# Rescheduling VectorE's work on batch 1 inside batch 0: fold pieces, evictions and two additions moved

## The chip, the cores and the metric

One core of a Trainium2 chip. The time is the device time of one execution in microseconds (us).

## The reference, cut to what matters

```python
X = np.fft.fft(np.fft.fft(x, axis=1), axis=2).real      # x: 8 x 3008 x 256
h = np.maximum(X^T @ w_tok1, 0) @ w_tok2                 # token mixing, per batch
u = X + h^T
out = u + np.maximum(u @ w_ch1, 0) @ w_ch2               # channel mixing, 1536 hidden
```

## The kernel before

Everything runs on TensorE as matmuls: the Fourier transform (`z`, `w`, `y`), the token product (`pt`, `pu`), the first channel product (`pc`) and the second (`po`, or seven products of half size, `pa` and `pb`). Other names in the traces: `ut` is the addition of token product and transform, on VectorE; `pad` is the last piece of the folded rows; `s` are sums of `c`, the evicted first product, for the seven products; a bank is one of the buffers into which TensorE writes, and an eviction empties it. The main loop goes through slots. A slot is one block of 128 hidden channels of the first channel product for one chunk of 512 rows; a chunk has 12 slots, a batch 72. Between the products of batch b the loop puts pieces of batch b+1's **front** (its transform and token mixing), and for batch 0 also what is left of its own front (`own`). Batch 1's rows must first be **folded** (sums and differences of mirrored rows): 26 pieces on VectorE in slots 12 to 29.

```python
for t0 in (11, 6, 1):                       # front: z from the folded rows eo
    for half in range(2):
        pz = ps_f("pz")
        ...
        copy(half == 0 and b > 0, zo[:, :, :, t0:t0 + 5], ...)   # True: VectorE, False: ScalarE
        yield
...
tt(ut[...], pu[...], yv, AT.add)            # token product + transform -> u, on VectorE
...
own_at = {..., 12: 1, 15: 1, 18: 1, 20: 1, 22: 1, 24: 1, 27: 1, 30: 1, 33: 1, 36: 1, 39: 1}
for b in range(BB):
    first = 24 if b == 0 else ...
    for c in range(NCH):
        on_v = ((1, 5, 8), ())[c] if b == 0 and c < 2 else () if joins else (0, 3, 6, 9)
        for ct in range(NCT):
            slot = NCT * c + ct
            mm1(b, c, c1, ct, on_v)         # two matmuls of 512 columns, one eviction with Relu
            ...                             # second product of the chunk before
            take(own, own_at.get(slot, 0))
            if 12 <= slot < 30:
                take(fold1, 1 + slot % 2)   # fold of batch 1
            if slot == 29:
                load_x(2)                   # GpSimd: loads of batch 2
            if 30 <= slot < 34:
                G.tensor_copy(out=w2r[...], in_=w2v[0][...])     # GpSimd: four copies
            while done < NFRONT * (slot + 1 - first) // (71 - first):
                take(nxt, 1)                # front of batch 1
```

Of the kernel before, what the change touches and what calls it, by code (L numbers as in the profile page):

```python
# [36 lines left out]
def kernel(  # L37
# [31 lines left out]
    def ps_f(name, dt=FP32, n=512):  # L69
        return psum.tile([P, n], dt, tag="f", name=name, bufs=3)  # L70
# [24 lines left out]
    def act(out_, in_, scale=1.0, func=AFT.Copy, bias=None):  # L95
        kw = {} if bias is None else {"bias": bias}
        nc.scalar.activation(out=out_, in_=in_, func=func, scale=scale, **kw)  # L97

    def copy(e, out_, in_):
        if e:  # L100
            V.tensor_copy(out=out_, in_=in_)
        else:
            act(out_, in_)
# [32 lines left out]
    def load_x(b):  # L136
        new_x(b)
        load_xp(b)
        for k in range(2):
            load_xm(b, k)  # L140
# [322 lines left out]
    def front(b):  # L463
# [5 lines left out]
        def stage1(out_, rows, half, tab, minus):  # L469
            if b:  # L470
                nc.tensor.matmul(out_, lhsT=rows[:, half * P:half * P + P], rhs=tab,  # L471
                                 start=True, stop=True)
                return
            for k in range(2):
                o = 129 * k + half
                nc.tensor.matmul(out_, lhsT=rows[:, o:o + P], rhs=minus if half and k else tab,
                                 start=k == 0, stop=k == 1)

        for t0 in (11, 6, 1):
            for half in range(2):  # L480
                pz = ps_f("pz")
                for k in range(5):
                    stage1(pz[:, 96 * k:96 * k + 96], eo[:, t0 + k], half, t1r, t1m[:])
                zo = z[:, half, :, :].rearrange("p k (u s) -> p u k s", u=4)
                copy(half == 0 and b > 0, zo[:, :, :, t0:t0 + 5],
                     pz[:, 0:480].rearrange("p (t u k) -> p u k t", t=5, u=4))
                yield
        for half in range(2):
# [10 lines left out]
            zo = z[:, half, :, :].rearrange("p k (u s) -> p u k s", u=4)[:, :, :, 0]  # L499
# [140 lines left out]
    def seven(b, c):  # L640
        if c == NCH - 1:
            return b % 2 == 1 and b < BB - 1
        return b > 0 or c >= 2

    def weight_sums():
        G.tensor_copy(out=wc2[:, :, D:D + 1], in_=wc2[:, :, P:P + 1])
        lo, hi = wc2[:, 0:NH], wc2[:, NH:NCT]
        b12 = lo[:, :, D:P:-1]
        G.tensor_copy(out=b22[:], in_=hi[:, :, D:P:-1])
        tt(t1w[:], b12, lo[:, :, 0:P], AT.subtract, G)  # L650
        tt(t2w[:], b22[:], t1w[:], AT.subtract, G)
        tt(t3w[:], b22[:], b12, AT.subtract, G)
        tt(t4w[:], hi[:, :, 0:P], t2w[:], AT.subtract, G)

    def mm1(b, c, c1, ct, on_v, cts=None):
        ut = state[b]["ut"]
        n = min(CW, S - CW * c)
        cts = cts or (ct,)
        pcs = [ps_out("pc", k % 5) if b + c == 0 and k % 5 < 2 else ps_mm("pc") for k in cts]
        for h in range(2):  # L660
            for pc, ct in zip(pcs, cts):
                nc.tensor.matmul(pc[:, 0:n], lhsT=wc1[:, h, ct * P:(ct + 1) * P],  # L662
                                 rhs=ut[:, c, h, 0:n], start=(h == 0), stop=(h == 1))
        for pc, ct in zip(pcs, cts):
            if ct not in on_v:
                act(c1[:, ct, 0:n], pc[:, 0:n], func=AFT.Relu)
            else:
                ts(c1[:, ct, 0:n], pc[:, 0:n], 0.0, AT.max)
# [3 lines left out]
    def turn_u(b, c):  # L672
        ut = state[b]["ut"]
        uT = work.tile([P, 4, 2, P], FP16, tag="uT", name="uT", bufs=3)
        n = CW if c < 5 or b % 2 else 384
        for h in range(2):
            nc.sync.dma_start_transpose(out=uT[:, 0:n // P, h, :], in_=ut[:, c, h, 0:n])
        return uT
# [18 lines left out]
    def sums(c1, box, k):  # L697
        a11, a12, a21, a22 = quads(c1)
        box[k] = work.tile([P, NH, 2, P], FP16, tag=f"s{k}", name=f"s{k}", bufs=1)
        if k == 1:  # L700
            tt(box[1][:], a21, a22, AT.add)
        elif k == 2:
            tt(box[2][:], box[1][:], a11, AT.subtract)
        elif k == 3:
            tt(box[3][:], a11, a21, AT.subtract)
        else:
            tt(box[4][:], a12, box[2][:], AT.subtract)
# [97 lines left out]
    def take(g, n):  # L805
        for _ in range(n):
            next(g, None)
# [12 lines left out]
    V.memset(td[:, 64:65], 0.0)  # L820
    take(fold0, 5)
    own = front(0)
    take(tu_q, 3)
    take(tu_p, 2)
# [15 lines left out]
    for k in range(4):  # L840
# [12 lines left out]
    hold = const.tile([P, 1], FP16, tag="hold")  # L853
    G.memset(sab[:, :, 1, 0:129:128], 0.0)
    own_at = {1: 1, 2: 1, 4: 1, 12: 1, 15: 1, 18: 1, 20: 1, 22: 1, 24: 1, 27: 1, 30: 1, 33: 1,
              36: 1, 39: 1}
    prev = uT = uT_next = None
    folding = left = 0
    for b in range(BB):
        nxt = front(b + 1) if b + 1 < BB else iter(())  # L860
        fold1 = fold(1, V) if b == 0 and BB > 1 else iter(())
        first, done = (24 if b == 0 else 5 + 12 * ((left + 5) // 6 - 1) if left else 0), 0
        for c in range(NCH):
            c1 = work.tile([P, NCT, CW], FP16, tag="c1", name="c1", bufs=2)
            if c == 5 and b % 2:
                G.tensor_copy(out=c1[:, :, 448:512], in_=tail1[:])
            box = {}
            joins = prev is not None and seven(*prev[0:2])
            on_v = ((1, 5, 8), ())[c] if b == 0 and c < 2 else () if joins else (0, 3, 6, 9)
            for ct in range(NCT):  # L870
                slot = NCT * c + ct
                if b == 0 and slot < 3:
                    if slot == 0:
                        mm1(b, c, c1, ct, on_v, range(3))
                else:
                    mm1(b, c, c1, ct, on_v)
                if b == 0 and slot in (4, 16):
                    uT = turn_u(b, c)
                if ct == (11 if b == 0 and c == 1 else 10) and (b, c) not in ((0, 0), (BB - 1, NCH - 1)):
                    uT_next = turn_u(*divmod(NCH * b + c + 1, NCH))  # L880
                if joins:
                    if ct in places:
                        mm2_seven(*prev, places[ct], pbox)
                    if ct in sum_at:
                        sums(prev[2], pbox, sum_at[ct])
                elif prev is not None and ct % 3 == 2:
                    mm2(*prev, ct // 3, pbox)
                if slot == 1 and b == 0:
                    weight_sums()
                if b == 0:  # L890
                    take(own, own_at.get(slot, 0))
                    if 12 <= slot < 30:
                        take(fold1, 1 + slot % 2)
                    if slot == 29 and BB > 2:
                        load_x(2)
                    if 30 <= slot < 34:
                        th, hb = (slot - 30) // 2, slot % 2
                        G.tensor_copy(out=w2r[:, th, 32 * hb:32 * hb + 32, 0:NQ],
                                      in_=w2v[0][:, th, 32 * hb:32 * hb + 32, :])
                while done < NFRONT * (slot + 1 - first) // (71 - first):  # L900
                    take(nxt, 1)
                    done += 1
                if ct == 5 and (left or done >= 8):
                    if not left and folding < b + 2 < BB:
                        folding, left, fold2 = b + 2, NFOLD, fold(b + 2, G)
                    if left:
                        if joins:
                            G.tensor_copy(out=hold[:], in_=pbox[3][:, 0, 0, 0:1])  # L908
                        n = min(left, 6 if c == 5 or b < 2 else 5)
                        take(fold2, n)  # L910
                        left -= n
                        if left == 0 and folding + 1 < BB:
                            load_x(folding + 1)
            if c == 5 and b % 2 == 0:
                G.tensor_copy(out=tail1[:], in_=c1[:, :, 384:448])
            prev, pbox, uT = (b, c, c1, uT), box, uT_next
# [32 lines left out]
```

## Time and profile before

| | before |
|---|---|
| time, median of 3 | 601.67 us (601.45 to 602.59) |
| TensorE busy | 97% of the span |
| VectorE, ScalarE, GpSimd busy | 75%, 65%, 43% |
| waits of TensorE after slot 0 above 0.3 us, start to start | 1.07 (slot 24), 0.42 (31), 0.59 (39), 0.48 (64) us |

The first matmul of slot 0 starts at 33.63 us; what is before it is setup. A matmul's shown length overlaps the next one's (0.38 us for 512 columns, with the next start 0.215 us on), so a wait of TensorE is read as the distance between two starts less the step that the trace has for that size. The lines of the page and the timelines are in the prediction.

### The profile page before, as it was taken

What the parts mean: (1) busy time and instruction counts of PE and PEld (TensorE: products, weight loads), DVE (VectorE), ACT (ScalarE), POOL (GpSimd) and SP (SyncE); (2) the same over time, 40 slices, a digit from 0 to 9 for tenths busy, and PEclk for the clock granted to TensorE, in tenths of its full rate; (3) what the DMA queues carried; (4) which work ended last, traced back from release to release, by engine and by line L of the source; (5) the groups of instructions that cost most, each with busy time, mean ns of one, the idle gap of its engine ahead of it and who ended that gap; (6) DMA issues with size and microseconds to landing.
All of it is one profiled execution on the core that took longest, in us unless ns stands there. A gap on an engine that the chain in (4) does not pass through costs nothing.

```text
span 599.8 us, 15331 instructions
## 1 busy us (share of the span) xinstructions
PE 582.5 (97%) x6273; PEld 417.8 (70%) x6273; DVE 449.5 (75%) x924; ACT 390.2 (65%) x753; POOL 255.1 (43%) x396
## 2 busy tenths in 40 slices
PE   3899999999999999999999999999999999999997
PEld 3756676677767776667767777677766777666776
DVE  8769879685898668766898668856688757966663
ACT  8764665478647865477656867568665786556662
POOL 8550545937555554626348444565555000000000
PEclk9999999999999999999999999999999999999999
DMA  8992822277138913394335753376133422323533
GB/s 158 207 192 61 170 50 53 61 149 119 37 71 121 149 37 68 78 181 54 68 84 91 135 89 55 67 147 113 37 60 80 93 55 55 77 61 77 93 72 88
DMA packets 83414, 55.69 MB, mean 93 GB/s; under 512 B 53778, under 2 KB 80082, under 8 KB 82578
## 3 DMA queue, kind: packets, MB, share of 16 engines
q1 hardware_dynamic: 76816, 36.82, 31.9%
q0 software_dynamic: 6208, 17.63, 16.2%
q8 instruction: 49, 0.80, 0.6%
q10 hardware_dynamic: 320, 0.26, 0.2%
q14 instruction: 21, 0.17, 0.1%
HBM read 35.26 MB, written 24.64 MB: 100 GB/s over the span
## 4 chain that ended last, share of the span: by engine, by line
PE 82%; DVE 1%; issue 0%; DVEq 0%
PE pc L662 36%; PE pa L712 17%; PE pb L712 13%; PE pu L566 6%; PE po L775 4%; PE pt L595 3%; PE pz L471 1%; PE py L538 1%; PE pw L512 1%; PE pw L508 1%; DVE s L90 1%; DVE osb L90 0%; DVE ut L90 0%; PE pz L496 0%; DVE q L90 0%
## 5 line engine op out<-in xcount | busy, mean ns | idle before, releaser
L97 ACT ACTIVATE c<-pc 128x512 f16<-128x512 f32 (+1 forms) x553 | 314.4, 591 | 156.2 <-PE pc L662 138.7
L662 PE MATMUL pc<-ut,wc 128*128 128x512 f16 (+1 forms) x1152 | 316.5, 374 | 1.2 <-DVE ut L90 1.2
L712 PEld LDWEIGHTS <-s 128*128 128x128 f16 x1968 | 123.5, 98 | 37.5 <-DVE s L90 0.6
L662 PEld LDWEIGHTS <-wc 128*128 128x128 f16 x1152 | 97.0, 98 | 50.7 <-issue 3.0
L712 PEld LDWEIGHTS <-c 128*128 128x128 f16 x1476 | 93.0, 97 | 27.8
L90 DVE TENSOR_TENSOR q<-pa,uT 128x256 f32<-128x256 f32 x123 | 52.5, 427 | 47.6 <-PE pa L712 47.5
L90 DVE TENSOR_TENSOR s<-c 128x1536 f16<-128x1536 f16 x82 | 80.7, 984 | 4.7 <-ACT c L97 4.7
L908 POOL COPY hold<-s 128x1 f16<-128x1 f16 x29 | 5.4, 187 | 173.5 <-DVE s L90 173.5
L90 DVE TENSOR_TENSOR osb<-pb,q 128x256 f32<-128x256 f32 x123 | 52.0, 422 | 23.8 <-PE pb L712 20.3
L90 DVE TENSOR_TENSOR ut<-pu,yt 128x512 f16<-128x512 f32 (+1 forms) x96 | 63.3, 672 | 0.8 <-PE pu L566 0.4
L90 POOL TENSOR_TENSOR eo<-sab 96x512 f16<-96x512 f16 x48 | 52.7, 1114 | 1.6
L566 PE MATMUL pu<-w2r,uu 128*128 128x512 f16 (+1 forms) x168 | 50.0, 379 | 0.3 <-DVE ut L90 0.3
L90 POOL TENSOR_TENSOR sab<-fa,fb 96x256 f16<-96x256 f16 (+1 forms) x72 | 46.7, 673 | 0.0
L90 DVE TENSOR_TENSOR s<-s,c 128x1536 f16<-128x1536 f16 x41 | 40.4, 986 | 0.0
L97 ACT ACTIVATE w<-pw 128x257 f16<-128x257 f32 x90 | 34.8, 387 | 8.4 <-PE pw L512 5.5
L90 DVE TENSOR_TENSOR s<-c,s 128x1536 f16<-128x1536 f16 x41 | 39.0, 952 | 0.0
L775 PE MATMUL po<-wc,c 128*128 128x256 f16 x288 | 35.4, 273 | 0.0
L712 PE MATMUL pb<-wc,c 128*128 128x128 f16 x492 | 34.4, 219 | 0.0
L712 PE MATMUL pa<-wc,c 128*128 128x128 f16 x492 | 34.4, 219 | 0.0
L712 PE MATMUL pa<-t2w,s 128*128 128x128 f16 x492 | 34.2, 219 | 0.1
L712 PE MATMUL pb<-t1w,s 128*128 128x128 f16 x492 | 34.2, 219 | 0.0
L712 PE MATMUL pa<-t4w,c 128*128 128x128 f16 x492 | 34.2, 219 | 0.0
(187 smaller groups left out, 728.0 us busy)
## 6 DMA issues: line engine op xcount, KB each, us to landing
out_dram<-osb SPq DMA_DIRECT2D x83, 256.0 KB
xp<-in_x_dram POOLq DMA_DIRECT2D x14, 408.0 KB, 6.4
out_dram<-osb SPq DMA_DIRECT2D x11, 192.0 KB
uT<-ut SPq DMA_TRANSPOSE x96
w2n<-in_moe_w_tok_dram POOLq DMA_DIRECT2D x2, 752.0 KB, 9.8
w1p<-in_moe_w_tok_dram POOLq DMA_DIRECT2D x2, 384.0 KB, 8.2
wc<-in_moe_w_ch_dram POOLq DMA_DIRECT2D x1, 768.0 KB, 15.3
xp<-in_x_dram POOLq DMA_DIRECT2D x2, 272.0 KB, 5.7
```

The costliest lines, as they stand in the source:

```text
L90: eng.tensor_tensor(out=out_, in0=a, in1=b, op=op)
L97: nc.scalar.activation(out=out_, in_=in_, func=func, scale=scale, **kw)
L471: nc.tensor.matmul(out_, lhsT=rows[:, half * P:half * P + P], rhs=tab, start=True, stop=True)
L508: nc.tensor.matmul(pw[:, 0:256].rearrange("p (h d) -> p h d", h=2)[:, :, 0:65], lhsT=zg[:, 0, g], rhs=td[:, 0:130].rearrange("p (h d) -> p ...
L512: nc.tensor.matmul(pw[:, 64:322].rearrange("p (h d) -> p h d", h=2)[:, :, 0:64], lhsT=zg[:, 1, g], rhs=td[:, 130:258].rearrange("p (h d) - ...
L538: nc.tensor.matmul(py[:, P * k:P * k + P], lhsT=w[:, 4 * c + k, o:o + P], rhs=tab[:, 4 * c + k, :], start=True, stop=True)
L566: nc.tensor.matmul(pu[:, 0:64 * nk], lhsT=uu[:, th, h, :], rhs=w2[:, th, :, 8 * c:8 * c + nk], start=(th == 0), stop=(th == 1))
L595: nc.tensor.matmul(pt[:, o:o + n], lhsT=hw[:, g, c], rhs=w[:, g, w0:w0 + n], start=(g == 0), stop=(g == NG - 1))
L662: nc.tensor.matmul(pc[:, 0:n], lhsT=wc1[:, h, ct * P:(ct + 1) * P], rhs=ut[:, c, h, 0:n], start=(h == 0), stop=(h == 1))
L712: nc.tensor.matmul(dst[:, P * a:P * a + P], lhsT=left[:, k, a, :], rhs=right[:, k, :], start=(first and k + a == 0), stop=(k == NH - 1), s ...
L775: nc.tensor.matmul(po[:, o:o + D], lhsT=c1[:, ct, ks * P:ks * P + P], rhs=wc2[:, ct, 0:D], start=(ct == 0), stop=(ct == NCT - 1))
L908: G.tensor_copy(out=hold[:], in_=pbox[3][:, 0, 0, 0:1])
```

## The change

The intent: take work from VectorE where TensorE waits for it. The fold gets one piece a slot up to slot 20 and two after; the front's start is moved from 24 to 25; batch 1's `z` and chunk 2's four VectorE evictions go to ScalarE; the last two additions of `own` go from slots 36 and 39 to 35 and 37.

```diff
-                copy(half == 0 and b > 0, zo[:, :, :, t0:t0 + 5],
+                copy(half == 0 and b > 1, zo[:, :, :, t0:t0 + 5],
...
-              36: 1, 39: 1}
+              35: 1, 37: 1}
...
-        first, done = (24 if b == 0 else ...), 0
+        first, done = (25 if b == 0 else ...), 0
...
-            on_v = ((1, 5, 8), ())[c] if b == 0 and c < 2 else () if joins else (0, 3, 6, 9)
+            on_v = ((1, 5, 8), (), ())[c] if b == 0 and c < 3 else () if joins else (0, 3, 6, 9)
...
-                        take(fold1, 1 + slot % 2)
+                        take(fold1, 1 if slot < 21 else 2)
```

More of the change, by code (lines that the diff above doesn't have):

```diff
@@ L861 @@
         fold1 = fold(1, V) if b == 0 and BB > 1 else iter(())
-        first, done = (24 if b == 0 else 5 + 12 * ((left + 5) // 6 - 1) if left else 0), 0
+        first, done = (25 if b == 0 else 5 + 12 * ((left + 5) // 6 - 1) if left else 0), 0
         for c in range(NCH):
```

## The prediction

> **What bounds the kernel now.** The profile's page comes first: which engine fills the span, and how much of the span it leaves open.
>
> ```profile
> span 599.8 us, 15331 instructions
> PE 582.5 (97%) x6273; PEld 417.8 (70%) x6273; DVE 449.5 (75%) x924; ACT 390.2 (65%) x753; POOL 255.1 (43%) x396
> ```
>
> TensorE sets the end: the chain that ended last is 82% PE. The change adds and removes no matmul, so it can only win back time in which TensorE waits. The second view is therefore the list of PE's waits (us in total, times, longest).
>
> ```profile
> PE filler L399 <- DVE ident L84: 8.1, 1, 8.1
> PE pc L662 <- DVE ut L90: 1.2, 2, 0.9
> ...
> PE pu L566 <- DVE ut L90: 0.7, 2, 0.4
> ...
> PE pz L496 <- DVE pad L90: 0.3, 1, 0.3
> ```
>
> The 8.1 us are the setup, which stays. What is left after about 33.6 us, where batch 0's slots begin (a slot is one block of 128 hidden channels of the first channel product, 12 to a chunk), is little, and all of it waits for VectorE. The third view, the timeline of PE, gives the places (start, length, then the instruction).
>
> ```profile
> 51.86 0.38 PE L662 MATMUL pc<-ut,wc 128*128 128x512 f16 x1
> 53.14 0.38 PE L662 MATMUL pc<-ut,wc 128*128 128x512 f16 x1 [0.90 <-DVE ut L90]
> ...
> 62.34 0.20 PE L496 MATMUL pz<-t1n,pad 96*128 96x24 f16 x2 [0.26 <-DVE pad L90]
> ...
> 71.13 0.59 PE L662 MATMUL pc<-ut,wc 128*128 128x512 f16 x2
> 72.15 0.64 PE L566 MATMUL pu<-w2n,uu 128*128 128x448 f16 x2 [0.42 <-DVE ut L90]
> ...
> 100.51 0.59 PE L566 MATMUL pu<-w2r,uu 128*128 128x512 f16 x2 [0.31 <-DVE ut L90]
> ```
>
> Matmuls of 512 columns follow each other every 0.215 us in this trace (two in 0.43), although each shows 0.38, so a delay is read from start to start. Slot 24: 53.14 - 51.86 - 0.215 = 1.07 us. Slot 31: 62.34 - (61.48 + 0.43) = 0.43. Slot 39: 72.15 - (71.13 + 0.43) = 0.59. Slot 64: 100.51 - (99.65 + 0.375) = 0.48. The sum is 2.57 us, 0.43% of the time: a ceiling for a change that touches batch 0 alone.
>
> The fourth view, the timelines of VectorE and GpSimd, says why VectorE is late.
>
> ```profile
> 42.12 0.77 DVE L90 TENSOR_TENSOR fa<-xp,xm 96x508 f16<-96x508 f16 x1 [2.67 <-DMA xm<-in_x_dram,ix]
> 42.81 1.76 DVE L90 TENSOR_TENSOR fb<-xm,xp 96x508 f16<-96x508 f16 x1
> ...
> 52.41 0.68 DVE L90 TENSOR_TENSOR ut<-pu,yt 128x512 f16<-128x512 f32 x1
> ...
> 68.48 3.08 DVE L90 TENSOR_TENSOR s<-c 128x1536 f16<-128x1536 f16 x1
> ```
> ```profile
> 61.55 1.10 POOL L106 DMA_DIRECT2D xp<-in_x_dram  x2 [17.27 <-DVE sab L90]
> ...
> 65.17 5.58 POOL L898 COPY w2r<-w2n 128x1504 f16<-128x1504 f16 x4
> ```
>
> The fold of batch 1 starts when its rows land, at 42.12, and from there to 53.14 VectorE is busy for 10.88 of 11.02 us. The ut that slot 24 needs is at the end of that queue. The sum s, usually 0.94 to 0.98 us, takes 3.08 because the four copies of w2r run on GpSimd until 70.75.
>
> [...]
>
> **The change part by part.** Durations below are steps from one start to the next in the trace of before.
>
> (a) The fold of 26 pieces (four row groups of six, then two for row 0). Before, slots 12 to 20 take 13 pieces and slots 12 to 22 take 16; after, 9 and 13. Within one slot the fold comes after the slot's own ut. So ahead of slot 22's ut stand pieces 1 to 15 before and 1 to 11 after. The four that move behind it are eo 0.34, fa 0.33, fb with its ends 0.45, the first sab pair 0.41: 1.53 us. That ut then starts at 52.41 - 1.53 = 50.88 and ends near 51.55. Its matmul ends at 50.26 (49.57 + 0.69), and the ut of slot 20 begins at 48.99 against a matmul end of 48.88, so neither gets a new wait. Slot 24's second matmul wants to start at 52.07: in time by 0.5 us. **The 1.07 us go.** PE's stream before 51.86 has nothing to win.
>
> (b) The pieces must still be early enough for batch 1's front. Continuing VectorE's queue with the rows' steps and with (c) taken out: ut of slot 24 ends at 54.34, of slot 27 at 57.22, piece 18 at 55.42, piece 24 at 58.30. PE, 1.07 us earlier, wants piece 17 at 56.40 and piece 23 (57.96) at 59.03. Both hold by a microsecond.
>
> (c) The z of batch 1 (three of 480 columns) and chunk 2's four evictions on ScalarE. VectorE is freed of 3 x about 0.6 + 4 x 0.6 = 4.2 us between slots 24 and 33; ScalarE gets 3 x 0.5 + 4 x 0.5 = 3.5 us. With that VectorE has caught up by slot 28: it then waits for slot 29's product (po ends 59.2), adds it (0.73), and does the last piece (0.41), at 60.34. PE wants that pad at 60.84. **The 0.43 us of slot 31 go**, with half a microsecond in hand. ScalarE: 53.14 to 68.09 shows 7.15 us busy out of 14.95; with 3.5 more it is under 11 of 13.4. In slots 25 to 30 it has 1.1 us a slot, 6.6 against PE's 7.6, and the slots short for it (0.64 us) come between long ones with 1.33 us of second product. With three banks for pc and three for pz and pu I find no place where PE arrives before the eviction.
>
> (d) "Its front a slot later": first goes from 24 to 25 in floor(46(slot + 1 - first) / (71 - first)). For slots 25 to 70 both give slot - 24. In slot 71 the new one asks for a 47th step of a generator that is done. So this part changes **nothing**.
>
> (e) The last two ut of batch 0 go from slots 36 and 39 to 35 and 37. Before, the one of 36 stands behind the sum s of 3.08 us and slot 39's matmul waits for its bank. After, the one of 35 is ahead of s. GpSimd's loads for batch 2 wait for fold piece 25, which ends near 58.8 instead of 61.3, so its w2r copies end near 68.2 instead of 70.75. s, reached at 67.4, then ends near 69.1 and the ut of 37 near 70.8 (0.35 + 0.87 + 0.55 on). PE needs the second sum at slot 41, near 71.6. **The 0.59 us go**, if slot 39 doesn't get the bank of slot 37's ut: PE is there at 70.55, 0.25 us too early. Before, two other banks took turns under ScalarE in such a stretch.
>
> The 0.48 us at 100.51 belong to batch 1's ut in slots 60 and on, whose order doesn't move. Later batches get the same program, and their start only shifts. Sum: 1.07 + 0.43 + 0.59 = 2.09 us; 601.67 - 2.09 = 599.6. I put 0.15 back for small new waits of the kind of (e): **599.75 us**.
>
> **The rivals.** First, ScalarE becomes the bound in slots 24 to 35: for it, 1.1 us a slot against PE's 0.64 in slots 25 and 28; against it, its 65% on the whole and the long slots between. It would cost up to a microsecond: 600.7. Second, [...]if its loads don't move up (they wait for landings too), s still ends at 71.5, the second sum at 73.2, and slot 41's product, wanted at 71.6, waits 1.6 us: 601.3, nearly all lost. The 17.27 us wait for sab ahead of the loads speaks against it. Third, slot 24's ut stays late, since slots 21 to 23 take two pieces each and the front of the queue is bound by the landing at 42.12: half of the first term lost, 600.3. Fourth, more is won than listed, because VectorE's slack also ends the 0.48 us: 599.1.
>
> **Range and chances.** The three terms are independent enough that losing one is likelier than losing all, and runs of before spread over 1.1 us. I take 598.9 to 601.2. Two per cent is 12 us: there isn't that much waiting after the setup, and ScalarE's 3.5 us cannot make it either. Faster by over 2%: 0.005; within: 0.985; slower: 0.01.
>
> **What would show each step.** In the changed profile: no gap at slot 24 with ut ending near 51.5 (a); none before the pad matmuls near 60.8 (b, c); ScalarE's share of the stretch to chunk 3 at about 80% with no "PE pc <- ACT c" in the waits (c); batch 1's front matmuls in the same slots as before (d); w2r copies starting near 62.7, s under 2 us, and no wait of pu or pw before chunk 3's first products (e). The 0.3 to 0.5 us before pu in slot 64 remain. I would be wrong if PE's list of waits showed ACT, or if a wait on s or ut stood near 71 us.

The second rival: "its loads" there are GpSimd's. The sum: 1.07 + 0.43 + 0.59 = 2.09 us, 601.67 - 2.09 = 599.58, and the 0.15 put back give 599.75 with the rounding. From the trace of before: fb took 1.76 us beside GpSimd's t4w (42.57 to 44.29 us) and 0.41 in other places; an eviction of 128x512 took 0.68 us on VectorE and 0.60 on ScalarE.

## The result, and the profile after

The changed kernel took 600.61 us (600.51 to 600.61, 3 runs) against 601.67. The ratio is 0.9978 with a 95% interval of 0.9955 to 1.0001. Ratios here are the mean time of one kernel's fast runs over that of the other's of the same rounds, so not quite the ratio of the medians. The page of the changed kernel begins:

```profile
span 598.5 us, 15332 instructions
PE 582.7 (97%) x6273; PEld 418.5 (70%) x6273; DVE 445.2 (74%) x917; ACT 393.9 (66%) x760; POOL 255.3 (43%) x396
```

Seven instructions went from VectorE to ScalarE (924 to 917, 753 to 760), as intended. The list of PE's waits (us in total, times, longest):

```profile
PE filler L399 <- DVE ident L84: 8.8, 1, 8.8
...
PE pu L566 <- DVE ut L90: 0.3, 1, 0.3
```

The waits of pc for ut and of pz for pad are gone from it; the one wait of pu left is slot 64's. The first line is in the setup, which the change doesn't touch, and is 0.7 us longer; more on that below. The timeline of PE at the places of the prediction:

```profile
52.43 0.59 PE L662 MATMUL pc<-ut,wc 128*128 128x512 f16 x2
...
61.42 0.20 PE L496 MATMUL pz<-t1n,pad 96*128 96x24 f16 x2
...
71.24 0.59 PE L662 MATMUL pc<-ut,wc 128*128 128x512 f16 x2
71.79 0.22 PE L508 MATMUL pw<-td,z 128*128 128x130 f16 x1
...
99.11 0.59 PE L566 MATMUL pu<-w2r,uu 128*128 128x512 f16 x2 [0.30 <-DVE ut L90]
```

At slot 24 the two matmuls now stand in one line (x2): they followed each other without a gap. The pad matmul has no bracket. At slot 40 pw starts 0.55 after pc where 0.43 is the step: a new wait of 0.12 us. Slot 64 keeps its 0.47. VectorE's and GpSimd's timelines, at the lines that answer to those of before:

```profile
51.36 0.68 DVE L90 TENSOR_TENSOR ut<-pu,yt 128x512 f16<-128x512 f32 x1
...
60.54 0.49 DVE L90 TENSOR_TENSOR pad<-sab 96x65 f16<-96x65 f16 x4
...
68.10 1.90 DVE L90 TENSOR_TENSOR s<-c 128x1536 f16<-128x1536 f16 x1
...
71.12 0.61 DVE L90 TENSOR_TENSOR ut<-pu,yt 128x448 f16<-128x448 f32 x1
```
```profile
60.00 1.10 POOL L106 DMA_DIRECT2D xp<-in_x_dram  x2 [16.03 <-DVE sab L90]
...
63.61 5.58 POOL L898 COPY w2r<-w2n 128x1504 f16<-128x1504 f16 x4
```

Slot 0 starts at 34.19 here and not at 33.63, so times are best compared from there. The ut that slot 24 needs starts 17.17 us after slot 0 (18.78 before). GpSimd's copies end 35.0 us after it (37.1 before), and the sum s, which ends 0.81 us after the last copy in both, is 1.90 us long and not 3.08.

From the first pc matmul to the end the profile has 566.14 us before and 564.32 after: **1.82 us less**. The spans differ by only 1.26, since the setup of this execution happened to be 0.56 longer.

**The setup's own spread.** Both programs have the same setup. In the timelines of VectorE, first of before, then of after, an instruction on one column shows where the two executions first part (the one in front of it, ix at 1.86, does the same: 0.94 and 1.72 us):

```profile
2.01 0.80 DVE L84 TENSOR_SCALAR icol<-pcol 128x1 f32<-128x1 f32 x1
```
```profile
2.01 1.58 DVE L84 TENSOR_SCALAR icol<-pcol 128x1 f32<-128x1 f32 x1
```

The one like it at 1.02 us (xicol) takes 0.15 us in both. In one case icol ends at 2.81, just after a GpSimd load's issue (1.41 to 2.68), in the other at 3.59, just after the iota that follows it (2.69 to 3.55). In all 14 profiles ident starts either at 7.7 or at 8.5 us, seven each, and two executions of the same instructions in the same order (the changed kernel and `front_24` below) fall on both sides; the kernels profiled twice fell on one side both times. This does not decide when slot 0 starts: with the early ident it starts at 33.56 to 34.78 us, with the late one at 34.08 to 34.30. Another difference lies in the setup's pz matmuls, which follow each other every 0.08 us at first and every 0.043 later: before has the shorter step at 13.4 us, the changed kernel from 14.4, `before_again` (slot 0 at 34.78) not yet at 15.0. What sets slot 0 stays open.

### The profile page after: what moved, and what is told of

Read it like the earlier page. It is cut to its first block, busy times and chain, and to the rows that moved or that the text cites. A ratio compares the mean times of both kernels' runs of the same rounds, so it can differ in the third digit from the quotient of the medians.

```text
span 598.5 us, 15332 instructions
## 1 busy us (share of the span) xinstructions
PE 582.7 (97%) x6273; PEld 418.5 (70%) x6273; DVE 445.2 (74%) x917; ACT 393.9 (66%) x760; POOL 255.3 (43%) x396
## 4 chain that ended last, share of the span: by engine, by line
PE 82%; DVE 1%; issue 0%; DVEq 0%
PE pc L662 35%; PE pa L712 17%; PE pb L712 13%; PE pu L566 6%; PE po L775 4%; PE pt L595 3%; PE py L538 1%; PE pz L471 1%; DVE s L90 1%; PE pw L512 1%; PE pw L508 1%; DVE osb L90 0%; DVE q L90 0%; DVE ut L90 0%; DVE z L101 0%
## 5 line engine op out<-in xcount | busy, mean ns | idle before, releaser
L90 DVE TENSOR_TENSOR s<-c 128x1536 f16<-128x1536 f16 x82 | 79.3, 968 | 4.7 <-ACT c L97 4.7
```

The lines of the kernel that those rows point to most:

```text
L90: eng.tensor_tensor(out=out_, in0=a, in1=b, op=op)
```

## The experiments

The theory: VectorE is one queue, full from the start of batch 1's fold until the pad piece (in before it is busy for 10.88 of the 11.02 us up to slot 24's second matmul); TensorE waits at the points where that queue delivers too late. Its order decides which point, its length whether there is one. The rival is that each part of the change wins its own term. Times are medians; "from slot 0" is from the first pc matmul to the last instruction of the profiled run. front_24, fold_only, scalar_only and slots_back shared their runs of before (602.90 us, 11 runs); so did slots_only, z_back, evict_back and fold_dose (602.12, 7 runs), and the last four (601.87, 9 runs, one of them of 604.91, which widens the intervals there). z_back, evict_back and fold_dose are compared with the changed kernel by their traces. They were run at other times. All results are correct.

**front_24: the changed kernel with the front's start put back**

```diff
-        first, done = (25 if b == 0 ...
+        first, done = (24 if b == 0 ...
```

> The changed kernel with first back at 24. Theory: the formula gives every front step the same slot, the instruction order of every engine is the same as of the changed kernel, so this is a second measurement of the changed kernel: ratio to before 0.997 to 0.998 (about 1.3 to 1.9 us faster), no wait at slots 24, 31 and 39, from the first pc matmul to the end 564.3 us within 0.2. Rival: the front a slot later matters, and some of the gain is missing here.

A comparison of the instruction order finds it the same on every engine (two neighbours in the setup, 0.11 us apart in one trace, are listed the other way round). 600.52 us, ratio 0.9965 (0.9951 to 0.9979). From slot 0 564.72 us, 0.4 more than expected: here pw at slot 40 waited 0.57 us. The fold had got going later in this run (see the table below). So this part does nothing, and the run is a second measurement of the change, which is now clear of noise.

**fold_only: the fold schedule alone**

```diff
-                        take(fold1, 1 + slot % 2)
+                        take(fold1, 1 if slot < 21 else 2)
```

> The kernel before with the new fold schedule alone. Theory (VectorE is one queue that is full from the landing of batch 1's rows to the pad piece): the 1.07 us at slot 24 go, but the pad piece ends as late as before, so PE waits 1.4 to 1.6 us in slots 27 to 31 in place of 0.43, and the 0.59 us at slot 39 stay: same time as before within 0.2 us. Rival (the fold schedule is what wins, each term by itself): 1.07 us faster, 0.43 us at slot 31.

603.43 us, ratio 1.0010 (0.9995 to 1.0025). The timeline of PE, its three lines with a wait between slots 24 and 36:

```profile
58.33 0.37 PE L471 MATMUL pz<-t1n,eo 96*128 96x96 f16 x5 [0.42 <-DVE z L101]
...
61.25 0.39 PE L471 MATMUL pz<-t1n,eo 96*128 96x96 f16 x5 [0.79 <-DVE eo L90]
...
63.68 0.39 PE L496 MATMUL pz<-t1n,pad 96*128 96x24 f16 x2 [0.44 <-DVE pad L90]
```

Slot 24 is left with 0.09 us. Three new waits came a little later, 0.59, 0.95 and 0.79 us from start to start: 2.33 in sum, more than the 1.07 + 0.42 of before, of which about 0.6 is a later start of the fold in this run. The sum foreseen was 1.4 to 1.6. Slot 39 kept 0.58, and from slot 0 the run took 567.10 us (566.14 before). A new order alone only moves the wait, as the theory says.

**scalar_only: z and evictions on ScalarE alone**

```diff
-                copy(half == 0 and b > 0, zo[...]
+                copy(half == 0 and b > 1, zo[...]
-            on_v = ((1, 5, 8), ())[c] if b == 0 and c < 2 else ...
+            on_v = ((1, 5, 8), (), ())[c] if b == 0 and c < 3 else ...
```

> The kernel before with z of batch 1 and chunk 2's evictions on ScalarE alone. Theory: 1.07 us at slot 24 stay, the 0.43 us at slot 31 go; GpSimd's loads start about 2 us earlier, the w2r copies end near 69 us, s is under 2 us long, and the 0.59 us at slot 39 go although its ut keeps its slot: 1.0 us faster. Rival (the slots of the ut win that term): 0.43 us faster, 0.5 us still at slot 39.

601.01 us, ratio 0.9972 (0.9957 to 0.9987). PE's only wait between slots 24 and 40:

```profile
53.95 0.38 PE L662 MATMUL pc<-ut,wc 128*128 128x512 f16 x1 [1.14 <-DVE ut L90]
```

It is 1.30 us from start to start. Slot 31's went, and slot 39's too, although its ut kept its place. VectorE's timeline shows why:

```profile
68.88 1.87 DVE L90 TENSOR_TENSOR s<-c 128x1536 f16<-128x1536 f16 x1
70.67 0.61 DVE L90 TENSOR_TENSOR ut<-pu,yt 128x448 f16<-128x448 f32 x1
```

The ut still stands behind s, but s is 1.2 us shorter: the copies end 35.7 us after slot 0, not 37.1. By the medians the run is 1.9 us faster, where 1.0 was expected; from slot 0 it took 565.44 us, 0.70 less than before, with a wait at slot 24 that is 0.23 longer. In time it can't be told from front_24 (601.01 and 600.52, intervals that overlap): what the fold schedule adds to it, the wait at slot 24, is shown by the traces alone.

**slots_only: the two additions in slots 35 and 37 alone**

```diff
-              36: 1, 39: 1}
+              35: 1, 37: 1}
```

> The kernel before with the last two ut in slots 35 and 37 alone. Theory (s is long because of the w2r copies, which end as late as before): the ut of slot 37 comes behind s and the second sum, near 40 us after the first pc matmul, and pw, two or three slots on, waits 1.0 to 1.9 us for its bank in place of 0.59 us at slot 39: 0.5 to 1.2 us slower than before. Rival, step (e) of the prediction: 0.59 us faster. Slots 24 and 31 as before.

602.36 us, ratio 1.0004 (0.9988 to 1.0021), from slot 0 566.40 (566.14 before). The timeline of PE:

```profile
73.74 0.22 PE L508 MATMUL pw<-td,z 128*128 128x130 f16 x1 [0.60 <-DVE ut L90]
```

That is slot 40, 0.76 us from start to start, in place of 0.59 at slot 39. By the trace, 0.26 us slower, the direction was right and the size was not (0.5 to 1.2 foreseen); the times show no difference. The reason: in working it out I had left the other ut between s and the next sum, from where the edit takes it, and so counted 0.53 us twice.

**slots_back: the changed kernel with the two additions back in 36 and 39** (run twice)

```diff
-              35: 1, 37: 1}
+              36: 1, 39: 1}
```

> The changed kernel with the last two ut back in slots 36 and 39. Theory: nothing is lost, because the w2r copies are what made s long and they end earlier here; the 0.12 us that pw waits at slot 40 go: from the first pc matmul to the end 564.1 to 564.3 us. Rival, my prediction's step (e): 0.4 to 0.6 us at slot 39 come back, 564.8 us.

600.25 us, ratio 0.9959 (0.9945 to 0.9973); from slot 0 564.13, with no wait at slots 24 to 40. Nothing is lost, so no gain from this part of the change is seen.

**z_back: the changed kernel with z back on VectorE**

```diff
-                copy(half == 0 and b > 1, zo[...]
+                copy(half == 0 and b > 0, zo[...]
```

> The changed kernel with the three z of batch 1 back on VectorE. Theory: 1.2 us of z (two of the three) stand ahead of the pad piece, whose slack in the changed kernel was 0.4 us: about 0.7 us of wait in slots 29 to 31, and w2r copies 1.2 us later, so a further 0.1 to 0.5 us near slot 40: 0.7 to 1.2 us slower than the changed kernel. Rival (the lead that the fold schedule gave covers the z): no wait, same time.

601.79 us, ratio 0.9996 (0.9979 to 1.0013). PE waits 0.61 us at slot 31 and 0.78 at slot 40; from slot 0 565.63, 1.31 more than the changed kernel.

**evict_back: the changed kernel with chunk 2's evictions back on VectorE**

```diff
-            on_v = ((1, 5, 8), (), ())[c] if b == 0 and c < 3 else ...
+            on_v = ((1, 5, 8), ())[c] if b == 0 and c < 2 else ...
```

> The changed kernel with four of chunk 2's evictions back on VectorE. Theory: two of them, 1.2 us, stand ahead of the pad piece: about 0.7 us of wait up to slot 31 and 0.1 to 0.5 us near slot 40; 0.7 to 1.2 us slower than the changed kernel. Rival: ScalarE had no room for them and the time gets better by up to 0.3 us.

601.75 us, ratio 0.9992 (0.9976 to 1.0009). 0.43 us at slot 29, 0.13 at slot 31, 0.77 at slot 40; from slot 0 565.52, 1.20 more. Both halves of the ScalarE part are needed: without either, two thirds of the 1.82 us or more are lost by the trace, because the lead at slot 31 was only 0.4 us.

**fold_dose: 14 pieces ahead of slot 22's addition**

```diff
-                        take(fold1, 1 if slot < 21 else 2)
+                        take(fold1, 1 if slot < 18 else 2)
```

> The changed kernel with two pieces a slot from slot 18 on, so that 14 pieces stand ahead of slot 22's ut (11 in the changed kernel, 15 before). Theory: the three more are 0.34 + 0.33 + 0.45 = 1.12 us against a slack of 0.6: 0.5 us of wait at slot 24 where the rows of batch 1 land as in the changed kernel's profile, and one for one more where they land later (0.5 to 1.7); slot 31 has no wait: 0.4 to 1.3 us slower than the changed kernel. Rival (any order with all 26 pieces done by slot 29 will do): same time.

600.90 us, ratio 0.9978 (0.9962 to 0.9995). The wait at slot 24 is back with 0.31 us, none at slot 31; from slot 0 564.54, 0.22 more than the changed kernel. So three pieces of 1.12 us used up a lead of 0.8, not 0.6: VectorE had itself stood idle a little for slot 20's matmul (0.1 us in the changed kernel's trace), which I had not counted; the other 0.1 is not explained. In time this run alone wouldn't show it.

**after_again and before_again: both kernels once more**

> The changed kernel once more, unchanged, beside the next three on one chip. Theory: 1.3 to 2.5 us faster than before; waits after slot 0 only at slot 40 (0.1 to 0.6 us, more where batch 1's rows land late after the first pc matmul), at slot 64 (0.48) and at batch 2's z (0.2 to 0.3). Rival: the 2.4 us of the first call of experiments came from a slow chip, and the gain is 1.1 us again.

> The kernel before, for a second profile. Theory: the waits at slots 24, 31 and 39 are there again, and if batch 1's rows land later after the first pc matmul than in the first profile, the wait at slot 24 is longer by the same amount (1.07 us plus the difference, within 0.1). Rival: the wait at slot 24 is a fixed 1.07 us.

The changed kernel: 600.51 us, ratio 0.9974 (0.9952 to 0.9996), 1.4 us by the medians. Before: one run of 602.28 (state unknown, being single). In its profile slot 24 waited only 0.21 us, slots 31 and 39 0.42 and 0.60. The fold got going earlier after slot 0: slot 0 itself was late (34.78 us), and fb ended 1.06 us earlier on the clock. The wait is not fixed, as the theory says. It fell by less than fb's end moved (0.86 against 2.2 us): VectorE started early and then stood idle for 1.25 us at slot 17 until the second product there was done. All profiles together, ordered within each order of the fold by the end of the first fb of batch 1, counted from slot 0:

| profile | order of the fold | slot 0 at | fb ends after it | wait at slot 24 |
|---|---|---|---|---|
| before_again | before | 34.78 | 8.74 | 0.21 |
| slots_only | before | 34.08 | 10.86 | 0.99 |
| before | before | 33.63 | 10.95 | 1.07 |
| scalar_only | before | 34.20 | 11.17 | 1.30 |
| fold_dose | 14 pieces ahead | 34.30 | 9.95 | 0.31 |
| after_again, after | after | 34.21, 34.19 | 9.89, 10.06 | 0 |
| z_back, evict_back | after | 34.11, 34.22 | 10.25, 10.83 | 0 |
| slots_back, slots_back_again | after | 34.04, 33.94 | 10.35, 10.82 | 0 |
| slot64, front_24 | after | 34.68, 33.56 | 11.26, 11.33 | 0 |
| fold_only | after | 34.22 | 11.53 | 0.09 |

In rows two to four, of the old order, the wait grows by 0.31 us while fb's end moves by 0.31. The new order takes every start seen here with at most 0.09 us of wait at slot 24.

What sets fb's end in these runs, by the traces, is GpSimd, and the prediction and the expectations, which speak of the rows' landing, miss that. When the weights wc have landed, GpSimd makes a row of products from them, up to t3w and t4w. Fold pieces beside these ended soon after them. In 13 of the 14 profiles fa ends 0.28 us after t3w and fb 0.28 us after t4w; in before_again fa itself ends 0.28 us after t4w. (These distances repeat within 0.01 us.) In before:

```profile
42.57 1.72 POOL L90 TENSOR_TENSOR t4w<-wc,t2w 128x768 f16<-128x768 f16 x1
```

t4w ends at 44.29 us and fb at 44.57. Without it fa and fb would be done near 42.9 (an estimate from 42.12 and their lengths elsewhere: a step of 0.34, then 0.41), so about 1.7 us of VectorE's full stretch is this hold. In the 13 profiles fb ends 7.73 to 7.75 us after GpSimd's first copy of wc, and that copy starts 2.1 to 3.8 us after slot 0 (0.8 in before_again). So it is the landing of wc that moved the fold, and with it the wait at slot 24, from one execution to the next. No run takes the products out of the way: what that would win is not tested.

The sum s beside the copies of w2r is the same kind of case. In all 14 profiles it ended 0.81 us after the last copy (71.56 and 70.75 us in before, 70.00 and 69.19 in the changed kernel), so an earlier end of the copies made it shorter: 3.08 us in before, 2.35 in front_24, 1.90 in the changed kernel, 1.87 in scalar_only, where the sums that follow take 0.94. It appears as busy throughout and not as idle time with a releaser: in before, VectorE's list of waits doesn't name GpSimd at all. By what means GpSimd's instructions make VectorE's longer is not shown. Landings vary too: over the 14 profiles batch 1's fold began, waiting for its rows, 6.6 to 9.3 us after slot 0.

**slots_back_again and slot64: a version that aims at the waits left**

slot64 is slots_back with two lines more, for the wait at slot 64:

```diff
-            V.tensor_copy(out=box["osb"][:, :, P:P + 1], ...)
+            copy((b, c) != (0, 3), box["osb"][:, :, P:P + 1], ...)
...
-                        n = min(left, 6 if c == 5 or b < 2 else 5)
+                        n = min(left, 6 if c == 5 or b < 2 and (b, c) != (0, 4) else 5)
```

> The changed kernel with the last two ut back in slots 36 and 39, beside the changed kernel. Theory: 0.1 to 0.6 us faster than the changed kernel, by its wait at slot 40, and no wait at slots 36 to 40. Rival: no difference, or slower.

> The last one, with two small things more for the wait at slot 64: one small column copy of VectorE there moved to ScalarE (it stands 0.87 us ahead of the first sum), and GpSimd's group of fold pieces in that chunk five instead of six (the sum was 1.29 us instead of 0.94 beside it). Theory: VectorE is 0.9 to 1.2 us earlier, the 0.48 us at slot 64 go, nothing else moves: 0.4 to 0.5 us faster than the one without. Rival: [...]ScalarE's wait for the product holds up evictions: same time or slower.

(Half of its rival is cut; it rested on a mechanism that no run shows.)

slots_back_again: 600.57 us, ratio 0.9973 (0.9952 to 0.9995), from slot 0 564.18 (changed kernel 564.36). slot64: 600.49 us, ratio 0.9970 (0.9947 to 0.9994), from slot 0 563.85. Its trace has no wait at slot 64, but 0.33 us at slot 39, where the late fold of that run put the copies and with them s (2.82 us long) later. The three kernels can't be told apart by their times (600.51, 600.57, 600.49); by the trace slot64 saves 0.5 us over the changed kernel and 0.3 over slots_back_again. It beats before as the others do, and that it beats the changed kernel in time is not shown.

## Why the prediction was right or wrong

The time, 600.61 us, lies in the range of 598.9 to 601.2; the point of 599.75 was 0.86 too low. Lying in the range says little about the steps: scalar_only (601.01), slots_back (600.25) and fold_dose (600.90) lie in it too, none of them with all the parts as changed. And as the old wait at slot 24 varies and the first call's ratio reaches 1.0001, landing this near the point is partly luck. Step by step:

- **(a) Right.** The ut for slot 24 was put at 50.88, 17.25 us after slot 0; it started 17.17 after it. The 1.07 us went. What the step took for a constant belongs to that execution, though, and the queue doesn't begin with the landing at 42.12 alone: fa and fb ended 0.28 us after GpSimd's t3w and t4w, fb at 44.57. The changed kernel's fb ended 0.9 us earlier after slot 0 than before's (10.06 against 10.95); VectorE then stood idle for 0.60 us at slot 17, so the ut came as foreseen all the same, and front_24, at 11.33, had no wait there either. With other starts of the fold the old kernel waits 0.21 to 1.07 us there, and one with its fold order 1.30. So the gain should vary from run to run; whether the ratios of the changed program (0.9978, 0.9965, 0.9974) and of slots_back (0.9959, 0.9973) differ for that reason is not shown, since their intervals overlap.
- **(b) Right.** No wait of pz for eo after slot 0.
- **(c) Right on the outcome.** The pad was foreseen 26.7 us after slot 0 and its last instruction ended at 26.8; PE wanted it at 27.2. z_back and evict_back show that both halves were needed. The sign for ScalarE was badly sized: I expected about 80% of the stretch up to chunk 3; it had 10.89 of 15.22 us, 72%. The 3.5 us added were about right (7.15 to 10.89), but I divided by a stretch of 13.4 us, having subtracted slot 24's wait, which was not in it, and left out the pu that moved into it. ScalarE held nothing up; the first rival fell.
- **(d) Right.** The order of instructions is the same with 24 and 25, on every engine.
- **(e) Outcome right, cause half wrong.** The 0.59 us went, but not through the slots: scalar_only loses them with the old slots, slots_back with the old slots keeps the gain, and slots_only makes the wait longer. What won was the other half of the step, GpSimd's copies ending 2.1 us earlier (35.0 us after slot 0, where 34.6 was foreseen). The warning that a matmul may get the bank of slot 37's ut came true, at slot 40 and not 39, with 0.12 us, and 0.57 in front_24, where the fold started late.
- **The sum.** 2.09 us were to be won and 0.15 given back. From slot 0 the profile has 1.82: 0.12 went at slot 40 and 0.12 more at a z of batch 2 on VectorE (0.17 before, 0.29 after).
- **The step that failed** is the last: taking the median of 601.67 as the place from which to subtract, with nothing set aside for setup. In the profiles the change's setup came out 0.56 us longer, which leaves 1.26 of the 1.82. With more runs of before (602.90, 602.12 and 601.87) the gain was 1.4 us beside after_again and 2.4 beside front_24. How much of the first call's 1.06 us is such chance can't be said: its timed runs left no traces.
- **"The three terms are independent enough"** was wrong. fold_only wins nothing, because the first term is only won if the second is too. The other way round it holds: scalar_only wins the second and the third without the first. The third rival, a late ut at slot 24, fell; the second, an s that still ends late beside GpSimd's copies, fell for the change but is what slots_only shows (s 2.54 us long, 0.76 us of wait at slot 40). The 0.48 us stayed, against the fourth.

## What to carry to other kernels

With VectorE's queue full over a stretch, a new order alone moved the wait along that stretch (fold_only: 2.33 us of waits in place of 1.07 + 0.42). Taking work off the queue (here 7 of its instructions, to an engine that was 65% busy) ended the two later waits, 0.42 and 0.59 us, by itself (scalar_only); the first one, ahead of the work that went, needed the new order, and that order without the lighter load only moved it. A wait that depended on when a DMA landed was not a constant (0.21 to 1.07 us at slot 24 in three profiles with the old order and load), and the DMA was one that another engine waited for, wc: read such a wait in more than one profile before subtracting it from a time. And look at what an earlier finish lets loose on another engine; here it was worth 0.59 of the 2.09 us aimed at.
